# A linear-attention block times a SwiGLU block: the first 512 + 512 tokens prepared in an order written out step by step, with ScalarE normalising

## The chip, the cores and the metric

One core of one Trainium2 chip. The metric is the device time of one execution in microseconds (us). All values are float32; the matmuls take them as pairs of fp32r values (a rounded "high" part and the "low" remainder). The engines: PE multiplies matrices, DVE (VectorE), ACT (ScalarE) and POOL (GpSimd) work elementwise, SP only issues DMAs.

## The reference, cut to what matters

```python
xn = layernorm(x)                                  # x: 2048 tokens x 1024
q, k, v = heads(xn @ wqkv)                         # 32 heads of 32
pq, pk = phi(q), phi(k)                            # phi(t) = where(t > 0, t + 1, exp(t)) + 1e-6
o = (pq @ (pk^T v)) / (pq . sum(pk) + 1e-6)
s = merge(o) @ wo
g = silu((silu(xn @ w1) * (xn @ w3)) @ w2)         # w1, w3: 1024 x 3584
out = x + s * g
```

## The kernel before

The tokens are worked on in two halves of 1024. In a half, all products with the normalised rows `xn` (keys, queries, gate, up) are computed as 2x2 block products with seven instead of eight multiplications (Strassen's scheme in Winograd's form). The blocks of the left operand are 512 tokens by 512 columns: A11 and A12 are the two column halves of the first 512 tokens (row tiles `xa0` to `xa3`, 128 tokens each), A21 and A22 those of the next 512 (`xb0` to `xb3`). The seven products use

- from the rows: A11, A12, A22, S1 = A21 + A22, S2 = S1 - A11, S3 = A11 - A21, S4 = A12 - S2;
- from a pair of 128-column weight blocks: B11, B21, B22, T1 = B12 - B11, T2 = B22 - T1, T3 = B22 - B12, T4 = B21 - T2.

The pairing is B11 with A11, B21 with A12, T2 with S2, T3 with S3, T1 with S1, T4 with A22, B22 with S4. PE needs the row blocks turned: four 128x128 transposes into one PSUM bank per block and row tile (tiles `tA..`, `tS..`, line 165). Then `split` (lines 95, 96) writes the high part by an ACT cast and the low part by a DVE subtraction. One product is 12 matmuls of 128x512: four blocks of the inner dimension times three combinations of high and low (`mm3`, lines 103 to 105).

The opening of the first half is what the change touches. Rows and weights come by DMA and must be normalised, summed, turned and split before PE can multiply at full pace. `prepare_first` loads the four `xa` tiles, takes their moments on DVE, normalises them on DVE (line 158), stores them (`keep_rows`, a DMA issued by POOL, line 175) and turns A11 and A12. `Operands.made(early=True)` loads the first weight columns of a key pair (`w0k`) and makes B11 and B21; the other columns come later with the whole pair (`wk`, line 327). `gemm(early=True)` runs B11 and B21 of each of the four key pairs, since these need only the `xa` rows. `prepare_rest` loads and normalises the `xb` tiles on DVE, makes S1, S3, S2, S4 on POOL (lines 213 to 216), stores them and turns five blocks a row tile. Only then come the other five products of each pair (`bk`: T2, `ck`: T3 and T4, `dk`: T1 and B22). Tile names carry the pair: `ak` of pair 0 is `ak0_0`, written `ak__347` in the profile.

The order in which a queue holds its instructions is set by a scheduler that goes by its own estimate of times, within what the code's `issue_after` marks forbid. After the opening, `catch_up` puts one step of the waiting side work (next rows, weight sums) behind each product; that part of the code is the same in both kernels.

Of the kernel before, what the change touches and what calls it, by code (L numbers as in the profile page):

```python
# [16 lines left out]
P = 128  # L17
C = 512
# [4 lines left out]
def tile_linear_attention_times_swiglu(  # L23
# [102 lines left out]
    def load_rows(rows, name):  # L126

        t = praw.tile([P, 2, D], F32, tag="raw", name=name)
        for c, r0 in enumerate(rows):
            nc.sync.dma_start(out=t[:, c], in_=x[r0:r0 + P, :])  # L130
        return t

    def moments(xs, dst):

        bs = st.tile([P, 2, 2, nc.vector.BN_STATS_DIM], F32, tag="bs", name="bs")
        for c, t in enumerate(xs):
            gather(t, bs[:, c])
        spread(bs, dst)

# [4 lines left out]
    def spread(bs, dst):  # L144
        n = dst.shape[1]
        v, y, u = (st.tile([P, 2], F32, tag=a, name=a)[:, :n] for a in "vyu")
        for c in range(n):
            nc.vector.bn_aggr(out=dst[:, c], in_=bs[:, c])
        nc.vector.tensor_scalar_add(v, dst[:, :, 1], 1e-5)
        nc.scalar.activation(y, v, AF.Sqrt)  # L150
        nc.vector.reciprocal(y, y)

        nc.vector.tensor_mul(u, y, y)
        nc.vector.scalar_tensor_tensor(u, u, -0.5, v, op0=ALU.mult, op1=ALU.mult)
        nc.vector.scalar_tensor_tensor(dst[:, :, 1], u, 1.5, y, op0=ALU.add, op1=ALU.mult)
# [4 lines left out]
    def turn_into(A, b, i, name):  # L160

        for n, src in b.items():
            p_ = bank(f"t{n}{name}")
            for k in range(ND // 2):
                turned = nc.tensor.transpose(p_[:, k * P:(k + 1) * P], src[:, k * P:(k + 1) * P], ident)
            low = split(A[n][:, :, :, i * P:(i + 1) * P], p_.rearrange("p (k s) -> p k s", k=ND // 2))
        return turned, low

# [8 lines left out]
    def prepare_first(A, mom):  # L177

        xs = []
        for g in range(TH // 4):  # L180
            t = load_rows([(2 * g + e) * P for e in range(2)], f"xa{g}")
            xs += [t[:, e] for e in range(2)]
            for i in (2 * g, 2 * g + 1):
                moments(xs[i:i + 1], mom[:, i:i + 1])
                normalise(xs[i], mom[:, i])
                keep_rows(0, i, "A11", xs[i])
                turn_into(A, {"A11": xs[i][:, :C]}, i, f"0_{i}")
        for i, t in enumerate(xs):
            _, low = turn_into(A, {"A12": t[:, C:]}, i, f"0_{i}")
        return xs, low  # L190

    def load_second(mom, g):

        ts = []
        for i in (2 * g, 2 * g + 1):
            ts.append(job_tile([P, D], f"xb{i}") if i < 3 else pb.tile([P, D], F32, tag="b", name=f"xb{i}"))
            nc.sync.dma_start(out=ts[-1], in_=x[C + i * P:C + (i + 1) * P, :])
        j = TH // 2 + 2 * g
        moments(ts, mom[:, j:j + 2])
        return ts  # L200

    def prepare_rest(A, mom, i, t0, seconds, behind):

        with ExitStack() as order:
            for mark in behind:
                order.enter_context(tc.issue_after(mark.ins))
            if i % 2 == 0:
                seconds += load_second(mom, i // 2)
            t1, s1 = seconds[i], small(f"S1x{i}")
            normalise(t1, mom[:, TH // 2 + i])  # L210

            a11, a12, a21, a22 = t0[:, :C], t0[:, C:], t1[:, :C], t1[:, C:]
            nc.gpsimd.tensor_add(out=s1, in0=a21, in1=a22)
            nc.gpsimd.tensor_sub(out=a21, in0=a11, in1=a21)
            nc.gpsimd.tensor_sub(out=a11, in0=s1, in1=a11)
            last = nc.gpsimd.tensor_sub(out=a12, in0=a12, in1=a11)
            for n, t in (("S1", s1), ("S3", t1), ("S2", t0)):
                keep_rows(0, i, n, t)
        behind.append(last)
        yield  # L220
        turned, _ = turn_into(A, {"S2": a11, "S3": a21, "S1": s1, "A22": a22, "S4": a12}, i, f"0_{i}")
        yield turned
# [90 lines left out]
    class Operands:  # L313
# [5 lines left out]
        def __init__(self, w, c0, name, early=False, second=False):  # L319
            self.w, self.c0, self.name, self.raw, self.next = w, c0, name, None, None  # L320
            self.B, self.second = {}, second
            self.stages = self.made(early)
# [10 lines left out]

        def made(self, early):
            K = ND // 2
            b = {}

            def halves(t):
                b.update(B11=t[:, :K, :P], B21=t[:, K:, :P])

            def ready(n):
                self.B[n] = pb.tile([P, 2, K, P], FR, tag="b", name=f"{n}{self.name}")
                split(self.B[n], b[n])

            def combine(n, i0, i1, there):
                b[n] = b[there]
                nc.vector.tensor_sub(out=b[n], in0=b[i0], in1=b[i1])

            if early:
                first = pb.tile([P, ND, P], F32, tag="b", name=f"w0{self.name}")  # L350
                nc.sync.dma_start(out=first, in_=columns(self.w, self.c0, P))
                halves(first)
                ready("B11")
                ready("B21")
                yield
            self.ask()

            ahead = self.next is not None and not early
            if ahead and not self.second:
                self.next.ask()  # L360
            halves(self.raw)
            b.update(B12=self.raw[:, :K, P:], B22=self.raw[:, K:, P:])
            if early:
                combine("T1", "B12", "B11", "B11")
                ready("T1")
                combine("T2", "B22", "T1", "T1")
                ready("T2")
                yield
                combine("T3", "B22", "B12", "B12")
                ready("T3")  # L370
                yield
            else:
                ready("B11")
                yield
                combine("T1", "B12", "B11", "B11")
                combine("T3", "B22", "B12", "B12")
                ready("T3")
                yield
                combine("T2", "B22", "T1", "T3")
                ready("T2")  # L380
                yield
                ready("T1")
                yield
                ready("B21")
                yield
            combine("T4", "B21", "T2", "T2")
            ready("T4")
            yield
            ready("B22")
# [43 lines left out]
    def gemm(B, A, use, early=False, paired=False, own=False):  # L433
# [13 lines left out]
        last = product(ba, B.upto("B11"), A["A11"], True)  # L447
        copied = nc.scalar.copy(out=u, in_=ba)
        if early:
            catch_up(copied, last)  # L450
            yield
            product(ba, B.upto("B21"), A["A12"], False)
            use(0, 0, ba)
            yield
            for _ in B.stages:
# [866 lines left out]
```

## Time and profile before

| | |
|---|---|
| median of 3 runs | 2339.35 us (2336.13 to 2340.17) |
| the profiled execution | 2340.79 us, span 2339.0 us |
| PE busy | 2296.4 us, 98% of the span, 10752 matmuls |
| DVE, ACT, POOL busy | 1778.8, 926.3, 691.1 us |
| PE busy in the first 73 us | 48.96 us, clock 0.88 of full |
| PE busy from 84 to 757 us | 669.91 of 673 us, clock 1.00 |

Outside its opening PE hardly ever waits, so a microsecond less in the rest's other engines is worth nothing. In the first 73 us it waits, and part of that time it multiplies at a reduced clock. A row of the timeline gives start, duration, engine, line of the kernel, operation, tiles written and read, shape, count, and in brackets the idle time before it with what ended it. A matmul's duration is longer than the step from one matmul to the next, because matmuls overlap in the array; work on PE is counted in steps.

### The profile page before, as it was taken

Reading aid. Unit: us, or ns where it says so; the run is one execution under the profiler, and the core shown is the slowest. Engines: PE = TensorE matmul, PEld = TensorE weight load, DVE = VectorE, ACT = ScalarE, POOL = GpSimd, SP = SyncE. Lnnn points to the kernel's source line nnn. Section 1 sums busy time; section 2 is a strip of 40 time slices with the busy share of each in tenths; the row PEclk is TensorE's granted clock in tenths of the full one; section 3 lists DMA queues with packets and bytes.
Section 4 is the critical chain, followed back from the end, with each engine's and each line's share of the span. In section 5 each row is a group of like instructions: output and inputs, shape, how many; then the busy total and the mean of one; then the engine's idle time right before and its main releaser. Section 6 shows DMA issues by size and latency. Waiting matters only on the chain.

```text
span 2339.0 us, 31747 instructions
## 1 busy us (share of the span) xinstructions
PE 2296.4 (98%) x10752; PEld 1880.5 (80%) x10752; DVE 1778.8 (76%) x2830; ACT 926.3 (40%) x1639; POOL 691.1 (30%) x854
## 2 busy tenths in 40 slices
PE   6999999999999999999999999999999999999998
PEld 5788888888888888777888888888887888888876
DVE  8887898888877876567867788887755566767798
ACT  5555333433232554434243333334323634342433
POOL 4220342477676221001423435342310000000033
PEclk9999999999999999999999999999999999999999
DMA  6555556576668746776666666665756565766688
GB/s 225 179 180 178 159 178 185 173 222 216 209 217 312 248 136 200 253 257 205 213 195 194 197 195 211 200 216 168 239 171 195 165 196 172 227 205 186 190 268 269
DMA packets 353698, 479.74 MB, mean 205 GB/s; under 512 B 24208, under 2 KB 262800, under 8 KB 353424
## 3 DMA queue, kind: packets, MB, share of 16 engines
q1 hardware_dynamic: 315808, 357.63, 48.6%
q0 software_dynamic: 37728, 120.09, 15.8%
q8 instruction: 84, 1.38, 0.2%
q14 instruction: 78, 0.64, 0.1%
HBM read 306.71 MB, written 174.59 MB: 206 GB/s over the span
## 4 chain that ended last, share of the span: by engine, by line
PE 69%; DVE 6%; issue 5%; DMA 5%; ACT 1%; POOL 0%; SPq 0%; DVEq 0%; ACTq 0%; POOLq 0%
PE g L103 2%; PE g L104 2%; PE g L105 2%; PE cB L103 1%; PE cB L105 1%; PE cB L104 1%; PE dB L105 1%; PE dB L103 1%; PE dB L104 1%; PE aB L105 1%; PE aB L103 1%; PE aB L104 1%; PE bB L105 1%; PE bB L103 1%; PE bB L104 1%
## 5 line engine op out<-in xcount | busy, mean ns | idle before, releaser
L751 POOL DMA_DIRECT2D h_d<-sg x112 | 83.0, 742 | 253.0 <-DVE sg L747 166.6
L1070 POOL DMA_DIRECT2D u_d<-uB x32 | 17.4, 542 | 404.1 <-DVE uB L1053 361.1
L96 DVE TENSOR_TENSOR xy<-xy,xy 128x512 fp32r<-128x512 f32 x112 | 73.1, 686 | 64.1 <-ACT xy L95 64.1
L95 ACT CAST xy<-xy 128x512 fp32r<-128x512 f32 x112 | 65.6, 621 | 101.2 <-PE g L105 57.5
L104 PE MATMUL g<-xy,xy 128*128 128x512 f32 x224 | 87.6, 391 | 0.2 <-DVE xy L96 0.2
L105 PE MATMUL g<-xy,xy 128*128 128x512 f32 x224 | 87.1, 390 | 0.0
L103 PE MATMUL g<-xy,xy 128*128 128x512 f32 x224 | 82.6, 398 | 0.0
L518 POOL DMA_DIRECT2D y_d<-y x48 | 34.7, 724 | 140.5 <-ACT y L538 80.6
L1053 DVE TENSOR_TENSOR acc<-cB,acc 128x512 f32<-128x512 f32 x50 | 34.5, 690 | 41.2 <-PE cB L105 41.2
L1053 DVE TENSOR_TENSOR acc<-dB,acc 128x512 f32<-128x512 f32 x56 | 38.6, 689 | 29.7 <-PE dB L105 29.5
L731 POOL TENSOR_TENSOR hs<-hs,sg 128x256 f32<-128x256 f32 x56 | 60.6, 1083 | 0.1
L733 POOL TENSOR_TENSOR hs<-sg 128x256 f32<-128x256 f32 x56 | 57.6, 1029 | 0.0
L103 PEld LDWEIGHTS g<-xy,xy 128*128 128x128 f32 x224 | 41.8, 187 | 14.4 <-issue 4.1
L889 POOL DMA_DIRECT2D qs_d<-qd x32 | 18.1, 567 | 117.4 <-DVE qd L885 71.1
L1184 POOL DMA_DIRECT2D s_d<-s x32 | 17.4, 543 | 117.9 <-DVE s L1053 69.9
L730 POOL TENSOR_TENSOR hs<-sg,sg 128x256 f32<-128x256 f32 x56 | 50.3, 898 | 1.2
L734 POOL TENSOR_TENSOR hs<-sg,hs 128x256 f32<-128x256 f32 x56 | 50.0, 893 | 1.4
L104 PEld LDWEIGHTS g<-xy,xy 128*128 128x128 f32 x224 | 42.1, 188 | 9.8 <-DVE xy L96 1.2
L766 POOL TENSOR_TENSOR w<-w 128x256 f32<-128x256 f32 x28 | 27.9, 997 | 74.5 <-DMA w<-in_B_w 74.5
L105 PEld LDWEIGHTS g<-xy,xy 128*128 128x128 f32 x224 | 42.1, 188 | 8.9
L759 POOL DMA_DIRECT2D h_d<-hs x60 | 46.0, 767 | 3.5 <-POOL hs L734 2.4
L95 ACT CAST XS4B<-rS4B 128x384 fp32r<-128x384 f32 (+1 forms) x40 | 19.7, 494 | 58.8 <-PE cB L105 41.6
(5315 smaller groups left out, 8303.5 us busy)
## 6 DMA issues: line engine op xcount, KB each, us to landing
h_d<-hs POOLq DMA_DIRECT2D x60, 256.0 KB, 3.4
h_d<-sg POOLq DMA_DIRECT2D x56, 256.0 KB, 3.6
w<-in_B_w SPq DMA_DIRECT2D x56, 256.0 KB
wt_d<-w SPq DMA_DIRECT2D x28, 512.0 KB
xy<-x_d SPq DMA_DIRECT2D x28, 512.0 KB
xy<-y_d SPq DMA_DIRECT2D x28, 512.0 KB
h_d<-hs SPq DMA_DIRECT2D x52, 256.0 KB
y_d<-y POOLq DMA_DIRECT2D x48, 256.0 KB, 3.0
```

Source lines behind the costliest of these rows:

```text
L95: nc.scalar.copy(out=hi, in_=src)
L96: return nc.vector.tensor_sub(out=lo, in0=src, in1=hi.bitcast(F32))
L103: nc.tensor.matmul(acc, lhsT=wh, rhs=ah, start=start, stop=False, skip_group_check=True)
L104: nc.tensor.matmul(acc, lhsT=wh, rhs=al, start=False, stop=False, skip_group_check=True)
L105: return nc.tensor.matmul(acc, lhsT=wl, rhs=ah, start=False, stop=stop, skip_group_check=True)
L730: e.tensor_add(out=s1, in0=a21, in1=a22)
L731: e.tensor_sub(out=s2, in0=s1, in1=a11)
L733: e.tensor_sub(out=s3, in0=a11, in1=a21)
L734: e.tensor_sub(out=s4, in0=a12, in1=s2)
L751: nc.gpsimd.dma_start(out=h_d[i][2 * h + c][:, 2 * n:4 * n + 2, k], in_=src)
L759: queue.dma_start(out=h_d[i][2 * h + c][:, 6 + 4 * e:10 + 4 * e, k], in_=o[e].rearrange("p (e s) -> p e s", s=P))
L1053: return V.tensor_add(out=c, in0=src, in1=c)
```

## The change

A table `OPENING` lists every step of the opening, some 250 of them, in one sequence; a small class runs them, and inside a `manual_schedule` block the queues of PE, ACT, DVE and POOL keep that order. Beside the order, these things change:

- The rows are normalised by ACT (`do_norm`, an Identity activation with scale and shift by token; the `xa` tiles in column halves) instead of DVE, but for `xa3`, which DVE still does. DVE makes the shift. The square roots are taken for two tiles at once, and all four `xb` tiles come before the first exponential.
- S1, S3, S2 and S4 are made by DVE (but for two of the S1, on POOL). In their place POOL subtracts eleven of the low parts of weight blocks, eight before and three after the first T2 product (`glow`), which DVE did.
- The last blocks of S4 are turned during the first pair's products.
- The weights of pairs 0 and 1 come as two loads of 128 columns (`w0k`, `w1k`); the pairs' first columns come in the order 0, 3, 2, 1, and the loads of all rows are issued among them.
- B11 and B21 of a pair run as whole products, pair by pair (0, 3, 2 B11; 3, 2, 0 B21; then 1).

The diff, cut to its core:

```diff
-    def prepare_first(A, mom):
-    def load_second(mom, g):
-    def prepare_rest(A, mom, i, t0, seconds, behind):
...
+    OPENING = """
+        stat xa0; stat xa1; var a0; stat xa2; root a0; scale a0; stat xa3; norm1 xa0; high k0 B11; turn A11
+        0; norm1 xa1; var a1; low k0 B11; root a1; turn A11 1; high A11 0; scale a1; norm2 xa0; low A11 0;
...
+    LOADED = [3, 2, 1]
+
+    class Opening:
...
+            for i in range(4):
+                self.rows(f"xa{i}", i * P)
+            keys[0].fetch(self.load)
+            for k, e in zip(LOADED, range(4)):
+                keys[k].fetch(self.load)
+                self.rows(f"xb{e}", C + e * P)
+            self.rows("xb3", C + 3 * P)
...
+        def do_scale(self, g):
+            m, c = self.group(g)
+            settle(m, *self.roots[g])
+            nc.vector.scalar_tensor_tensor(self.shift[:, c], m[:, :, 0], -1.0, m[:, :, 1], op0=ALU.mult, op1=ALU.mult)
+
+        def do_vnorm(self, n):
+            normalise(self.x[n], self.mom[:, self.at(n)])
+
+        def do_norm(self, n, cols=slice(None)):
+            t, j = self.x[n][:, cols], self.at(n)
+            nc.scalar.activation(t, t, AF.Identity, scale=self.mom[:, j, 1:2], bias=self.shift[:, j:j + 1])
...
+        def do_high(self, n, i):
+            if n[0] == "k":
+                self.jobs[n, i] = self.keys[int(n[1])].place(i)
+            dst, src = self.jobs[n, i]
+            nc.scalar.copy(out=dst[:, 0], in_=src)
+
+        def do_low(self, n, i, e=nc.vector):
+            dst, src = self.jobs.pop((n, i))
+            return e.tensor_sub(out=dst[:, 1], in0=src, in1=dst[:, 0].bitcast(F32))
+
+        def do_glow(self, n, i):
+            self.do_low(n, i, nc.gpsimd)
+
+        def do_sum(self, n, i, e=nc.vector):
+            if n[0] == "k":
+                return self.keys[int(n[1])].combine(i)
+            i = int(i)
+            if n == "S1":
+                self.S1[i] = small(f"S1x{i}")
+                e.tensor_add(out=self.S1[i], in0=self.part("A21", i), in1=self.part("A22", i))
+            else:
+                a, b = {"S3": ("A11", "A21"), "S2": ("S1", "A11"), "S4": ("A12", "S2")}[n]
+                e.tensor_sub(out=self.part(n, i), in0=self.part(a, i), in1=self.part(b, i))
...
+        def do_mul(self, k, *_):
+            next(self.gemms[int(k[1])])
+
+        do_copy = do_relu = do_exp = do_phi = do_add = do_mul
...
+        def fetch(self, load):
+            first = pb.tile([P, ND, P], F32, tag="b", name=f"w0{self.name}")
+            load(first, columns(self.w, self.c0, P))
+            self.halves(first, 1)
+
+        def ask_rest(self, load):
+            self.raw = pb.tile([P, ND, P], F32, tag="b", name=f"w1{self.name}")
+            load(self.raw, columns(self.w, self.c0 + P, P))
+            self.halves(self.raw, 2)
...
-            m = [keys(pair, early=True, own=pair == 0) for pair in range(ND // 2)]
...
+            m = [keys(pair, early=True, own=pair == 0, led=pair == 0) for pair in range(ND // 2)]
+            some = mybir.EngineType
+            with tc.manual_schedule(engines={some.PE, some.Activation, some.DVE, some.Pool}):
+                last = Opening(A, early, m).run()
```

What it does to the queues is seen best on PE just ahead of the first T2 product. Before, all five blocks of the last row tile (`tS20_3`: S2 of tile 3, `xb3`, `S1x3`) stand there, S4 of every tile among them:

```order
L165 MATMUL tA220_2_669<-ident_63,xb2_468 128x128 x4
L165 MATMUL tS40_2_676<-ident_63,xa1_263 128x128 x4
L165 MATMUL tS20_3_683<-ident_63,xa1_263 128x128 x4
L165 MATMUL tS30_3_690<-ident_63,xb3_470 128x128 x4
L165 MATMUL tS10_3_697<-ident_63,S1x3_497 128x128 x4
L165 MATMUL tA220_3_704<-ident_63,xb3_470 128x128 x4
L165 MATMUL tS40_3_711<-ident_63,xa1_263 128x128 x4
L103 MATMUL bk0_0__739<-S2_0_209,T2k0_0__725 128x512
```

Now, at the same place on PE (`bk0_0` is again the T2 product of pair 0, `ak0_1` the B21 product of pair 1):

```order
L105 MATMUL ak0_1__569<-A12_0_212,B21k0_1__560 128x512
L272 MATMUL tA220_2_653<-ident_63,xb2_223 128x128 x4
L272 MATMUL tS20_2_660<-ident_63,xa1_220 128x128 x4
L272 MATMUL tA220_3_669<-ident_63,xb3_224 128x128 x4
L272 MATMUL tS40_0_675<-ident_63,xa0_219 128x128 x4
L272 MATMUL tS10_2_681<-ident_63,S1x2_558 128x128 x4
L272 MATMUL tS30_2_688<-ident_63,xb2_223 128x128 x4
L272 MATMUL tS40_3_694<-ident_63,xa1_220 128x128 x4
L103 MATMUL bk0_0__701<-S2_0_209,T2k0_0__643 128x512
```

All eight first products stand ahead of the T2 product in both, but 18 of the 20 second-row tiles are turned between them now; S4 of tiles 2 and 1 has moved behind it, the former here, between T3 and T1:

```order
L105 MATMUL ck0_0__702<-S3_0_210,T3k0_0__646 128x512
L272 MATMUL tS40_2_747<-ident_63,xa1_220 128x128 x4
L103 MATMUL dk0_0__703<-S1_0_211,T1k0_0__468 128x512
```

On POOL before, in the stretch after the four stores of the `xa` rows, the sums of one row tile stand between the stores of their results:

```order
L175 DMA x_d0_164<-xa1_263 128x1024 x2
L213 TENSOR_TENSOR S1x0_450<-xb0_430 128x512
L214 TENSOR_TENSOR xb0_430<-xa0_216,xb0_430 128x512
L175 DMA x_d0_164<-S1x0_450 128x512
L215 TENSOR_TENSOR xa0_216<-S1x0_450,xa0_216 128x512
L175 DMA x_d0_164<-xb0_430 128x1024
L216 TENSOR_TENSOR xa0_216<-xa0_216 128x512
```

Now POOL's queue at that place holds low parts of weight blocks (`B21k0_3` is B21 of key pair 3), and the only sum in it is an S1:

```order
L160 DMA x_d0_164<-xa0_219 128x1024
L284 TENSOR_TENSOR B21k0_3__365<-w0k0_3__231,B21k0_3__365 128x512
L284 TENSOR_TENSOR B11k0_2__371<-w0k0_2__234,B11k0_2__371 128x512
L284 TENSOR_TENSOR B21k0_0__374<-w0k0_0__229,B21k0_0__374 128x512
L284 TENSOR_TENSOR B11k0_1__404<-w0k0_1__237,B11k0_1__404 128x512
L160 DMA x_d0_164<-S1x1_459 128x512
L160 DMA x_d0_164<-xb1_222 128x1024
L295 TENSOR_TENSOR S1x0_502<-xb0_221 128x512
```

The sums have gone to DVE, where they stand between the low parts of the row blocks (line 284) now; a piece of DVE's queue:

```order
L284 TENSOR_TENSOR S2_0_209<-tS20_1_490,S2_0_209 128x4x128
L298 TENSOR_TENSOR xb0_221<-xa0_219,xb0_221 128x512
L298 TENSOR_TENSOR xa0_219<-S1x0_502,xa0_219 128x512
L295 TENSOR_TENSOR S1x3_531<-xb3_224 128x512
L298 TENSOR_TENSOR xb3_224<-xa1_220,xb3_224 128x512
L298 TENSOR_TENSOR xa1_220<-S1x3_531,xa1_220 128x512
L284 TENSOR_TENSOR S3_0_210<-tS30_0_526,S3_0_210 128x4x128
```

Before, DVE's queue held none of these sums; it held the normalisations of line 158 in their place.

More of the change, by code (lines that the diff above doesn't have):

```diff
@@ L192, in load_second @@
-    def load_second(mom, g):
[L194 to L200, printed above, removed]
-    def prepare_rest(A, mom, i, t0, seconds, behind):
[L204 to L222, printed above, removed]
@@ L332, in upto, with halves @@
             return self.B[n]
-        def made(self, early):
[L335 to L347, printed above, removed]
-            if early:
[L350 to L358, printed above, removed]
+        def halves(self, t, e):
+            K = ND // 2
+            self.b.update({f"B1{e}": t[:, :K], f"B2{e}": t[:, K:]})
@@ L447, in gemm @@
         last = product(ba, B.upto("B11"), A["A11"], True)
+        if early:
+            yield
         copied = nc.scalar.copy(out=u, in_=ba)
         if early:
-            catch_up(copied, last)
             yield
             product(ba, B.upto("B21"), A["A12"], False)
-            use(0, 0, ba)
             yield
-            for _ in B.stages:
-                pass
+            yield from use.steps(0, 0, ba)
+            yield
         else:
@@ L524, in use, with steps @@
         def use(n, c, src):
+            for _ in steps(n, c, src):
+                pass
+        def steps(n, c, src):
             j = 2 * pair + n
@@ L557, in turn @@
                 keep_keys(h, pair, "R6", rows["y00"])
+        use.steps = steps
         return use
@@ L697, in half @@
         if h == 0:
-            for g in m:
-                run(g)
+            with tc.issue_after(last.ins):
+                for g in m:
+                    run(g)
         else:
```

245 lines of the change are left out of this document (162 added, 83 removed).

## The prediction, made before the run

> **What bounds the kernel now.** I read the busy shares first, then the windows of the opening and of a steady stretch (length, then busy time and rows of PE, weight load, DVE, ACT, POOL, then PE's granted clock, DMA share and GB/s), then PE's waits of the first 75 us:
>
> ```profile
> PE 2296.4 (98%) x10752; PEld 1880.5 (80%) x10752; DVE 1778.8 (76%) x2830; ACT 926.3 (40%) x1639; POOL 691.1 (30%) x854
> 0.00:73.00 73.00, 48.96 (x223) 40.58 (x224) 61.29 (x132) 35.37 (x63) 30.47 (x38) 0.88 0.61 217
> 84.00:757.00 673.00, 669.91 (x3010) 553.50 (x3009) 553.91 (x783) 266.04 (x449) 319.49 (x386) 1.00 0.63 202
> PE tA L165 <- DVE v L149: 11.9, 1, 11.9
> PE bk__739 L103 <- ACT S L95: 4.7, 1, 4.7
> PE tS L165 <- DVE pk L508: 2.9, 1, 2.9
> PE tA L165 <- DVE xa L158: 1.7, 2, 0.9
> ```
>
> PE is full from 84 to 757 us and waits in the opening. So the change is worth what it takes out of the opening, less what it breaks later. PE's timeline prices PE's work:
>
> ```profile
> 11.90 1.09 PE L165 MATMUL tA<-ident,xa 128*128 128x128 f32 x4 [11.90 <-DVE v L149]
> 15.83 5.38 PE L165 MATMUL tA<-ident,xa 128*128 128x128 f32 x24 [0.80 <-DVE xa L158]
> 20.87 0.78 PE L103 MATMUL ak__347<-A,B11k__340 128*128 128x512 f32 x1
> ...
> 27.36 0.39 PE L103 MATMUL ak__347<-A,B21k__343 128*128 128x512 f32 x1
> 29.86 0.39 PE L105 MATMUL ak__347<-A,B21k__343 128*128 128x512 f32 x1
> 38.51 0.60 PE L165 MATMUL tS<-ident,xb 128*128 128x128 f32 x4
> 38.94 0.60 PE L165 MATMUL tS<-ident,S1x 128*128 128x128 f32 x4
> 65.59 0.79 PE L103 MATMUL bk__739<-S,T2k__725 128*128 128x512 f32 x1 [4.73 <-ACT S L95]
> 72.41 0.63 PE L103 MATMUL dk__741<-S,T1k__721 128*128 128x512 f32 x1
> 72.84 0.53 PE L104 MATMUL ck__740<-S,T3k__729 128*128 128x512 f32 x1
> 60.00:70.00 10.00, 4.53 (x16) 3.12 (x15) 9.20 (x16) 5.33 (x10) 0.72 (x2) 0.64 0.28 104
> ```
>
> 27.36 and 29.86 are the first and last of a product's twelve matmuls: 2.50 us for eleven steps, 0.227 each. A tile of four transposes is a step of 0.435 (38.51 to 38.94); in the first transposes, at a slow clock, 5.38 us for six tiles, 0.9 each. At 72.41 a matmul still takes 0.43.
>
> Call X the first T2 product, at 65.59. Before X stand 28 tiles (12.2 us at full clock) and eight products, 96 matmuls (21.8): 34.0 of work in 65.59, so 31.6 are lost. From X to 72.84 stand 14 matmuls, 3.2 of work in 7.25, because the 4.73 us of waiting ahead of X had let the clock fall (0.64 granted between 60 and 70): 4.1 lost. Together 35.7 us are lost. The window from 60 to 70 tells why: DVE busy 9.20 of 10, POOL 0.72. PE waits for DVE's list while POOL has nothing left. The order puts exactly the same products ahead of X after the change, but two tiles fewer.
>
> **The start.** DVE's moments, two rows of which group both halves of a tile, its small operations, and a cast on ACT:
>
> ```profile
> 5.73 1.23 DVE L142 BATCH_NORM_STATS2 bs<-xa 128x6 f32<-128x512 f32 x2
> 7.00 0.21 DVE L148 BATCH_NORM_AGGREGATE mom<-bs 128x2 f32<-128x12 f32 x1
> 7.81 1.29 DVE L142 BATCH_NORM_STATS2 bs<-xa 128x6 f32<-128x512 f32 x2 [0.60 <-DMA xa<-in_A_x]
> 10.94 0.81 DVE L158 TENSOR_SCALAR xa<-xa,mom 128x1024 f32<-128x1024 f32 x1
> 29.49 0.16 DVE L153 TENSOR_TENSOR u<-y 128x2 f32<-128x2 f32 x1
> 29.69 0.16 DVE L154 SCALAR_TENSOR_TENSOR u<-u,v 128x2 f32<-128x2 f32 x1
> 16.60 0.62 ACT L95 CAST B11k__363<-w0k__361 128x512 fp32r<-128x512 f32 x1 [0.94 <-DMA w0k__361<-in_A_wqkv]
> ```
>
> Roots for two tiles wait for the second tile's moments (5.73 + 1.23 = 6.96). The order also puts `xa2`'s moments ahead of the rest: 7.81 + 1.29 + 0.2 = 9.3. Five dependent small operations at a step of 0.2 (29.49 to 29.69): 10.3. Half a row's normalisation on ACT isn't in the trace; from below it is half of DVE's 0.81 for 1024, from above nearly the 0.62 of a 512-wide cast, which I take: 10.9. First tile turned at 11.0 instead of 11.90, a gain of 0.9. Three tiles at 0.9 end at 13.7. The fourth needs `xa3`'s moments (10.3 + 1.5), a low part (0.6), five small operations (1.0) and its normalisation (0.6): 14.4. Three more tiles: 17.1. A cast (0.6) and a low part (0.7) follow, and behind that cast on ACT stands the last half row (`norm2 xa1`); its tile and the first product come at **19.0**, where 20.87 stood.
>
> From 19.0 PE has eight products (21.8) and 18 tiles (7.8) to X: 29.6, so 48.6 if it never waits.
>
> **DVE up to X.** By the order DVE has in that stretch 37 passes of 128x512: low parts, weight sums, S sums; besides, the moments of three of the four `xb` tiles and 14 small operations.
>
> ```profile
> 60.08 0.68 DVE L347 TENSOR_TENSOR wk__718<-wk__718 128x512 f32<-128x512 f32 x1
> 60.68 0.68 DVE L96 TENSOR_TENSOR A<-tA,A 128x512 fp32r<-128x512 f32 x1
> 36.05 0.58 POOL L175 DMA_DIRECT2D x_d<-S1x  x1
> 36.65 1.31 POOL L215 TENSOR_TENSOR xa<-S1x,xa 128x512 f32<-128x512 f32 x1
> 38.46 1.29 POOL L216 TENSOR_TENSOR xa<-xa 128x512 f32<-128x512 f32 x1
> L1066 POOL TENSOR_TENSOR acc<-acc,uB 128x512 f32<-128x512 f32 x10 | 17.8, 1779 | 28.8 <-ACT acc L1211 16.1 <-DVE uB L1053 9.8 <-DVE acc L1053 2.9
> ```
>
> A pass is a step of 0.60 (60.08 to 60.68): 37 x 0.60 = 22.2; 3 x 1.4 = 4.2; 14 x 0.2 = 2.8; together 29.2. From the first product's low part at 18.4 this ends at 47.6, beside PE's 48.6. The normalisations are gone from DVE (seven of 0.81) and the POOL sums have come to it; that DVE now finishes near PE, not 17 us later, comes from the earlier start of the list, and from sums no longer waiting for POOL's chain of one tile after another (36.65, 38.46 with stores of 0.58 between).
>
> POOL gets eight low parts and two S1 ahead of X: 10 x 1.29 = 12.9, and 11 stores at 0.57, 6.3: 19.2 of about 35 us, so POOL is not the bound at that price. Its price for a subtraction with a rounded result isn't in the trace; 1.29 (38.46) is the nearest row, 1.78 the contended group's mean. The latter would make 17.8 + 6.3 = 24.1, still within 35.
>
> **DVE and POOL at once.** In the trace the two hold each other up:
>
> ```profile
> 36.93 1.05 DVE L153 TENSOR_TENSOR u<-y 128x2 f32<-128x2 f32 x1
> 38.21 2.79 DVE L155 SCALAR_TENSOR_TENSOR mom<-u,y 128x2 f32<-128x2 f32 x1
> 41.04 4.33 DVE L158 TENSOR_SCALAR xb<-xb,mom 128x1024 f32<-128x1024 f32 x2
> 600.00:620.00 20.00, 19.03 (x84) 15.46 (x83) 18.07 (x17) 5.48 (x11) 18.58 (x22) 1.00 0.71 236
> 608.52 0.68 DVE L464 TENSOR_TENSOR ug__5184<-bg__5206,ug__5184 128x512 f32<-128x512 f32 x1
> 610.90 2.46 DVE L347 TENSOR_TENSOR wu__5014<-wu__5014 128x512 f32<-128x512 f32 x1
> ```
>
> A 128x2 operation lasts 1.05 from 36.93 to 37.98, where POOL's sum of 36.65 + 1.31 ends (37.96); another lasts 2.79; a pass at 610.90 with both inputs in SBUF lasts 2.46, while one at 608.52 that reads PSUM for one input lasts 0.68. So a DVE operation with two SBUF inputs waits while POOL reads. Of the 29.2 us on DVE, 18 passes and 12 small operations (13.2, 45%) are of that kind. Bounds: none of POOL's 12.9 us meets one, cost 0; all of it does, cost 12.9. In proportion it is 45%, **5.8 us**. If instead every such pass met POOL as the one at 610.90 did (1.78 over 0.68, in a window with POOL busy 18.58 of 20, where here its operations fill 12.9 of 35), it would be 18 x 1.78 x 0.37/0.93 = 12.7, the upper end again. I take the proportional value, since neighbouring passes there, as at 608.52, lost nothing. So X comes at 47.6 + 5.8 + 0.6 for the last cast and turn = **54**.
>
> [...]
>
> **After X.** 14 matmuls (3.2), two S4 tiles moved there (0.9) and 1.5 for short waits bring PE at 59.6 to where it stood at 72.84: 13.2 us gained. The matmuls behind X need DVE's low part of the last S2 tile and POOL's of T2; a wait for either is in the 1.5. [...]
>
> [...]
>
> Loads:
>
> ```profile
> 25.10 0.63 ACT L95 CAST B11k__409<-w0k__407 128x512 fp32r<-128x512 f32 x1
> 18.57 0.37 SPq L351 DMA_DIRECT2D w0k__407<-in_A_wqkv  x1
> 759.97 0.50 PE L103 MATMUL bk__6503<-S,T2k__6354 128*128 128x512 f32 x1 [1.49 <-ACT T2k__6354 L95]
> ```
>
> Pair 0's second columns are asked for once POOL has done `B21k3` (about 21.5); a load asked for at 18.57 was used at 25.10, so it takes at most 6.5 us, 28.0. DVE wants it for T1 at about 27: 0 to 1 us, inside the 1.5. ACT loses nothing: its windows above show it about half busy. Later the code is the same with its order shifted a little, so I count one more wait like the row at 759.97 (1.5). Gain 13.2 - 1.5 = **11.7**.
>
> **Rivals.**
> R1, the strict lock: every microsecond of POOL's 12.9 falls on a DVE operation, 7.1 more than counted: 2334.8. For it, the 2.46 at 610.90; against it, DVE's 55% of other operations go on meanwhile.
> R2, slower: POOL's rounding subtraction has no row and takes d us. PE's products need these low parts, eight before X, so each costs d - 1.3 once POOL is full. POOL's spare time is 35 - 19.2 = 15.8; the gain is spent when 8 x (d - 1.3) exceeds 15.8 + 11.7, from d = 4.7 on. At d = 6 it is 37.6 - 15.8 = 21.8 lost against the forecast: 2349.5. Against it: rounding costs DVE nothing (0.68 at 60.08 without, 0.68 at 60.68 with it).
> R3, nothing waits: X near PE's own 48.6, 5.4 more gain: 2322.3. For it, POOL could fall beside DVE's PSUM reads.
> R4, the rest gives back 5: later sums and T4 are made when POOL is busy, as at 600 to 620, and waits like 759.97 come three more times: 2332.7.
> That the table isn't kept is excluded by the order, which shows it on all four queues.
>
> **How the numbers follow.** The profiled execution took 2340.79 us (span 2339.0), 1.44 above the median of the runs shown and just outside them. 2340.79 - 11.7 = 2329.1; carried to the median, 2339.35 - 11.7 = **2327.7**. Chances: forecast 0.52 (its own range 2324 to 2331), R1 0.14, R2 0.10, R3 0.12, R4 0.12. About 0.2%, 4.7 us, is what a measurement of this kernel can tell from no change, so faster means below 2334.7. The forecast, R3, half of R1 and two thirds of R4 are faster: 0.52 + 0.12 + 0.07 + 0.08 = 0.79. The rest of R1 and R4, 0.11, is the same, R2's 0.10 slower. The range reaches from a little under R3 to a little over R1, 2320 to 2337, and leaves R2 and a few extremes out.
>
> **What would show it.** Right: first transposes at about 11, first product near 19, X near 54, no PE wait over 2 us between 19 and X, 0.39-long matmuls right behind X, POOL subtractions near 1.3, DVE sums between 0.6 and 2, and no new PE waits from 84 to 757. Wrong in one term: X after 60 with DVE full and sums over 2 (R1); PE waiting for a POOL low part (R2); X under 50 (R3); PE waits of several us later (R4). A first product after 21 would put the start wrong, with whatever ACT holds there as the cause.

## The result, and the profile after

| | before | after |
|---|---|---|
| median of 22 runs each | 2339.22 us (2334.34 to 2343.51) | 2334.24 us (2328.17 to 2336.82) |
| the profiled execution | 2340.79 us, span 2339.0 | 2331.29 us, span 2329.5 |

The ratio is 0.9977 (95% interval 0.9972 to 0.9983): 5.0 us faster. Forecast were 11.7 us. The direction was right, the size was not half of it. 2334.24 is near what R4 (2332.7) and R1 (2334.8) gave. R1 it wasn't, since the first T2 product came well before 60; R4's mechanism has a part in it.

Busy shares and two windows of the changed kernel, in the same columns as before:

```profile
PE 2290.6 (98%) x10752; PEld 1873.7 (80%) x10752; DVE 1773.4 (76%) x2820; ACT 929.1 (40%) x1645; POOL 681.6 (29%) x851
```

```profile
0.00:73.00 73.00, 53.61 (x272) 43.13 (x273) 63.99 (x136) 43.39 (x75) 26.68 (x35) 1.00 0.62 217
84.00:757.00 673.00, 669.03 (x3000) 551.70 (x2999) 558.35 (x781) 267.51 (x454) 324.58 (x394) 1.00 0.64 206
```

In the opening PE is busy 4.7 us more and its granted clock is full where it was 0.88 (its record begins at 16.2 us, that of before at 21.9; ahead of that a transpose steps by 0.21 us in both kernels, where later it steps by 0.11). From 84 to 757 us it idles 4.0 us where it idled 3.1. PE's waits and its timeline:

```profile
PE tA L272 <- ACT xa L261: 12.7, 4, 11.4
PE tS L272 <- DVE A L284: 4.3, 2, 3.0
PE bk__6806 L103 <- ACT T2k__6622 L95: 1.3, 1, 1.3
```

```profile
11.40 1.09 PE L272 MATMUL tA<-ident,xa 128*128 128x128 f32 x4 [11.40 <-ACT xa L261]
...
18.79 0.47 PE L103 MATMUL ak__350<-A,B11k__268 128*128 128x512 f32 x1
...
48.06 1.16 PE L272 MATMUL tS<-ident,S1x 128*128 128x128 f32 x8 [2.98 <-DVE A L284]
...
56.57 0.50 PE L103 MATMUL bk__701<-S,T2k__643 128*128 128x512 f32 x1
56.91 0.39 PE L104 MATMUL bk__701<-S,T2k__643 128*128 128x512 f32 x1
```

The first tile is turned at 11.40 (forecast 11.0), the first product runs at 18.79 (19.0), the first T2 product X at 56.57 (54), and the matmul behind X takes 0.39, at a granted clock of 1.00. The start holds, X is 2.6 us late, and ahead of X stands a wait of 2.98 us. Its cause stands in DVE's and POOL's timelines:

```profile
43.95 3.37 DVE L284 TENSOR_TENSOR T1k__468<-w0k__229,T1k__468 128x512 fp32r<-128x512 f32 x1
47.24 1.27 DVE L284 TENSOR_TENSOR A<-tA,A 128x512 fp32r<-128x512 f32 x2
...
53.27 0.69 DVE L632 SCALAR_TENSOR_TENSOR pk<-ak__350,pk 128x512 f32<-128x512 f32 x1 [0.97 <-ACT pk L630]
...
55.23 0.69 DVE L284 TENSOR_TENSOR A<-tA,A 128x512 fp32r<-128x512 f32 x1 [1.07 <-ACT A L280]
55.84 0.68 DVE L284 TENSOR_TENSOR S<-tS,S 128x512 fp32r<-128x512 f32 x1
```

```profile
44.26 1.28 POOL L284 TENSOR_TENSOR B21k__560<-w0k__237,B21k__560 128x512 fp32r<-128x512 f32 x1
45.49 1.26 POOL L284 TENSOR_TENSOR B22k__582<-w1k__395,B22k__582 128x512 fp32r<-128x512 f32 x1
```

DVE's low part of T1, both inputs in SBUF, lasts 3.37 instead of 0.69: it ends at 47.32, 0.57 after POOL's two subtractions (to 46.75), as if it had begun only then. Behind it in DVE's queue stand the low parts of A22 (47.24), which free the PSUM banks that PE's next tiles need.

Where time went in the whole program I read from PE's records: from the start of PE's k-th matmul I take 0.2266 us for each 512-wide matmul before it and 0.109 for each transpose (0.435/4) and each narrower one. The rest is lost time. In the last part this price does not fit the narrower matmuls, so the differences count there, not the sign. The order of the last part (from the 3862nd matmul) is the same in both kernels. Three profiles of each kernel (the second and third from runs described below):

```
                      lost up to the 300th   300th to 3862nd     3862nd to the last
before                36.0  35.3  35.5       8.6   5.5   7.8     -39.1 -38.9 -40.0
after                 24.7  25.9  24.4       9.5  10.8  11.1     -37.7 -38.2 -38.2
gain of the means     10.6                   -3.2                -1.3
```

10.6 - 3.2 - 1.3 = 6.1; the means of the three spans (2337.2 and 2331.0) differ by 6.2. The forecast had 13.2 for the first column and -1.5 for the other two.

### The profile page after: what moved, and what is told of

Its sections match the earlier page's. It is cut to its first block, busy times and chain, and to the rows that moved or that the text cites. A ratio compares the mean times of both kernels' runs of the same rounds, so it can differ in the third digit from the quotient of the medians.

```text
span 2329.5 us, 31760 instructions
## 1 busy us (share of the span) xinstructions
PE 2290.6 (98%) x10752; PEld 1873.7 (80%) x10752; DVE 1773.4 (76%) x2820; ACT 929.1 (40%) x1645; POOL 681.6 (29%) x851
## 4 chain that ended last, share of the span: by engine, by line
PE 59%; DVE 4%; DMA 3%; issue 1%; ACT 1%; SPq 0%; DVEq 0%; ACTq 0%
PE g L103 2%; PE g L104 2%; PE g L105 2%; PE cB L103 1%; PE dB L105 1%; PE dB L103 1%; PE cB L105 1%; PE dB L104 1%; PE cB L104 1%; PE aB L105 1%; PE aB L104 1%; PE aB L103 1%; DMA rA22B<-h_d 1%; PE bB L103 1%; PE bB L105 1%
## 5 line engine op out<-in xcount | busy, mean ns | idle before, releaser
L642 POOL DMA_DIRECT2D y_d<-y x48 | 34.9, 727 | 117.1 <-ACT y L666 69.6
L1174 DVE TENSOR_TENSOR acc<-dB,acc 128x512 f32<-128x512 f32 x56 | 38.5, 688 | 30.1 <-PE dB L105 29.9
L104 PEld LDWEIGHTS g<-xy,xy 128*128 128x128 f32 x224 | 42.1, 188 | 10.6 <-DVE xy L96 1.5
L798 POOL DMA_DIRECT2D pq_d<-pq x32 | 17.5, 547 | 104.5 <-DVE pq L632 104.3
```

What stands on the lines that cost most here:

```text
L104: nc.tensor.matmul(acc, lhsT=wh, rhs=al, start=False, stop=False, skip_group_check=True)
L1174: return V.tensor_add(out=c, in0=src, in1=c)
```

## The experiments

**The same kernels again.** No edit. Two theories of the 3 us between the profiled execution and the median:

> The changed kernel unchanged, for a second profile and more times with PE's granted clock of each. The profiled execution took 2331.29 us with a mean granted clock of 0.999, and its first T2 product came at 56.6 us as forecast (54), yet the median of 22 runs is 2334.24. Theory A (clock): in most executions PE's waits of the opening (3.0 us at 45 to 48 above all) let the clock fall, which the first profile happened to escape. Then a profile with a mean clock of 0.997 or 0.998 shows matmul steps of 0.43 instead of 0.227 somewhere before 75 us, 5 to 10 us of them, and the time of a run goes with its clock, about 2.3 us for each 0.001. Rival B (later waits): the opening is the same in every execution, and the 3 us lie in PE's waits behind 300 us, at the change of halves (740 to 790) above all; then steps in the opening stay at 0.227 and the later waits grow by 3 us or more.

> The kernel before unchanged, for a second profile and the clock of each run. [...] Rival B: its opening is the same to 0.5 us and its spread comes from later waits.

Medians 2334.72 (11 runs) and 2338.24 (10). The second profile of the changed kernel (2333.59 us), PE's timeline behind the wait and two windows:

```profile
47.94 1.94 PE L272 MATMUL tS<-ident,S1x 128*128 128x128 f32 x8 [2.98 <-DVE A L284]
49.53 0.78 PE L103 MATMUL ak__569<-A,B21k__560 128*128 128x512 f32 x1
50.10 0.63 PE L104 MATMUL ak__569<-A,B21k__560 128*128 128x512 f32 x1
50.53 0.63 PE L105 MATMUL ak__569<-A,B21k__560 128*128 128x512 f32 x1
50.95 0.43 PE L103 MATMUL ak__569<-A,B21k__560 128*128 128x512 f32 x1
```

```profile
45.00:55.00 10.00, 7.06 (x38) 6.38 (x39) 7.77 (x12) 4.79 (x9) 3.90 (x4) 0.83 0.28 111
745.00:755.00 10.00, 7.99 (x27) 5.83 (x26) 9.91 (x10) 5.09 (x10) 7.72 (x9) 0.83 1.03 376
```

After the same 2.98 us wait the clock falls here and matmuls step by 0.43 (50.10 to 50.53); in the first profile, and in the third, they don't (granted from 45 to 55: 0.83 here, 1.00 there). Once more it falls at the change of halves (745 to 755, granted 0.83), where seven steps of 0.43 cost 1.4 us. So both theories hold a part: the clock is one source of the spread, with about as much at the change of halves (1.4 us) as in the opening (1.2 more lost up to the 300th matmul). Among the 22 runs the two at a mean clock of 0.999 took 2328.2 and 2331.3, the ten at 0.998 2333.9 in the median, the eight at 0.997 2335.1, the two at 0.996 2332.9 and 2336.8. In the 11 runs of the second series the time does not go with the clock: 2333.4 at 0.999, but 2333.2 and 2336.1 at 0.996. The kernel before is nearer to rival B: its opening differs by 0.7 us between profiles, its later waits by 3.2.

**The pass that collided.** In the list of steps (here and below cut to the steps that change):

```diff
-        0; low k0 T1; exp k3;
+        0; exp k3;
-        phi k0; high A22 2;
+        phi k0; low k0 T1; high A22 2;
```

> DVE's low part of T1 of pair 0, which took 3.37 us at 43.95 behind two POOL subtractions, stands ten steps later, behind the feature map of pair 0, where DVE was idle; nothing else changes. Theory A: PE's wait of 3.0 us before the S1 tiles of rows 0 and 3 falls to under 0.6, the first T2 product comes 2 to 2.7 us sooner (near 54), the clock stays at full in more executions, and the median falls by 3 to 6 us, to 2328 to 2331. Rival B: only the wait goes, the median falls by 2 to 2.7 us, to 2331.5 to 2332.3. If later waits take it all back, the median stays at 2334.

T1's low part is taken from a block here that T2's sum has overwritten, so this part of the computation is another; the operations are the same. X came at 53.37, 3.2 us sooner, lost time to the 300th matmul was 21.5 (25.0 in the mean of the changed kernel), the median 2331.24, between what theory A and rival B had. PE's wait in the place was gone. That is more than the 2.7 that the pass lasts too long, but the pass itself also stands now where DVE had idled. The run with both edits, further down, keeps it among the busy passes and loses 22.7 up to the 300th matmul: by it the collision alone costs the opening 2.3 us.

**POOL's low parts back to DVE.**

```diff
-        B11; high k3 B21; low k3 B11; high A12 3; low A12 2; glow k3 B21; high k2 B11; low A12 0; high k0
+        B11; high k3 B21; low k3 B11; high A12 3; low A12 2; low k3 B21; high k2 B11; low A12 0; high k0
...
```

and so at all eleven places.

> The eleven low parts that the change gave to POOL go back to DVE, at the same places of the list. My sum for the opening holds that POOL's eight before the first T2 product cost DVE 5.8 us of blocked passes (the traces show 2.7 in one pass and some 3 in small ones), and DVE would pay 8 x 0.60 = 4.8 for doing them itself. So by my terms it comes out about even: first T2 product within 2 us of 56.6, the median 2333 to 2337. If POOL's parts cost DVE nearly nothing but the one pass, it is slower by 2 to 4 us in the opening (2336 to 2339).

A miss: X at 54.42, lost time 22.6, median 2329.88 (ratio to before 0.9964, 0.9950 to 0.9979), so 4.8 us under the changed kernel on the same chip (2334.72) and not even with it. The T1 pass in DVE's timeline, and X in PE's:

```profile
43.82 0.68 DVE L284 TENSOR_TENSOR T1k__468<-w0k__229,T1k__468 128x512 fp32r<-128x512 f32 x1
```

```profile
54.42 0.50 PE L103 MATMUL bk__701<-S,T2k__643 128*128 128x512 f32 x1
```

DVE does 4.8 us more before X and yet is done sooner. From 18.3 us to X its steps add up to 34.9 us here and to 34.8 in the changed kernel, but it idles 1.0 instead of 3.4. So this part of the change costs time in the opening: what POOL takes from DVE's list it gives back in held-up passes, and more through what waits for them. The opening explains 2.4 of the 4.8. Between the 300th and the 3862nd matmul this profile lost 12.4, more than the changed kernel's, so where the rest of the 4.8 comes from is not shown.

**One place of the second half in its old order.** Line 95's cast of T2 for the second key pair of the second half, on ACT and DVE:

```diff
-                phi(src, pq)
+                with ExitStack() as held:
+                    if (h, pair, n, c) == (1, 0, 1, 0):
+                        held.enter_context(tc.issue_after(cast["k1_1_"].ins))
+                    phi(src, pq)
...
```

`cast` keeps the instruction that casts a pair's T2. In the same way the copy of `k1_1_` and the two operations that make `y10` and R5 of pair 0 are held behind T2's cast and low part.

> The changed kernel, with one place of the unchanged second half put back into the order that it had in the kernel before: on ACT the copy of the B11 product, the turned keys' bias and the feature map of the last query block stand behind the cast of the next key pair's T2, on DVE the difference R5 behind T2's low part. In both profiles of the changed kernel PE waits 1.3 us there (near 786), in both of the kernel before it doesn't. Theory O (the order of the rest): the wait goes, the second half starts its next pair 1.3 us sooner, and the median falls by 1.0 to 1.6, to about 2333.2. Rival: the engines are late there whatever the order, because the queries of the pair come late; then the wait moves to the next product and the median stays at 2334.5.

In the changed kernel PE waits for this cast, and the cast stands behind a copy and a bias; first PE's and then ACT's timeline:

```profile
787.24 0.50 PE L103 MATMUL bk__6806<-S,T2k__6622 128*128 128x512 f32 x1 [1.33 <-ACT T2k__6622 L95]
```

```profile
785.51 0.59 ACT L556 COPY uk__6776<-ak__6777 128x512 f32<-128x512 f32 x1 [0.45 <-PE ak__6777 L105]
785.99 0.69 ACT L673 ACTIVATE y<-trk,tiny 128x512 f32<-128x512 f32 x1
786.57 0.62 ACT L95 CAST T2k__6622<-wk__6558 128x512 fp32r<-128x512 f32 x1
```

With the old order restored, the same matmul in PE's timeline has no wait ahead of it:

```profile
786.70 0.60 PE L644 MATMUL trk<-ident,pk 128*128 128x128 f32 x4
787.39 0.50 PE L103 MATMUL bk__6806<-S,T2k__6622 128*128 128x512 f32 x1
```

The third profile of the changed kernel comes to the same place at the same time:

```profile
786.72 0.60 PE L638 MATMUL trk<-ident,pk 128*128 128x128 f32 x4
788.65 0.50 PE L103 MATMUL bk__6806<-S,T2k__6622 128*128 128x512 f32 x1 [1.33 <-ACT T2k__6622 L95]
```

From the 3300th to the 3500th matmul the three profiles of the changed kernel lost 2.2, 1.8 and 1.8 us, those of before 0.2, this one 0.5. So the written opening changes what the scheduler does 700 us later, in code that the diff doesn't touch, and at this place that costs 1.3 us: shown. That the whole program gets it back is not shown. The median was 2332.83 (0.9968, 0.9958 to 0.9979), 1.4 to 1.9 under the changed kernel, but on another chip, the interval overlaps the changed kernel's (0.9972 to 0.9983), and the profiled execution (2333.54) is no shorter than the mean of the changed kernel's three (2332.8).

**Both edits**, with T1's low part ahead of T2's sum this time:

```diff
-        0; low k0 T1; exp k3;
+        0; exp k3;
-        sum k0 T2; high S2 3;
+        high S2 3;
-        low S2 3; high S1 3;
+        low S2 3; low k0 T1; sum k0 T2; high S1 3;
```

> The edit of the run before (one place of the second half in the old order) and in the opening DVE's low part of T1 behind the low part of S2 of tile 3, with the weight sum of T2 right behind it, where POOL has no subtraction left to hold it up. The pass of 3.37 us falls to about 0.7, PE's wait of 3.0 us to under 0.6. By waits alone: 2.6 from the opening and 1.3 from the second half, 2334.5 to 2330.6. If the slow clock behind that wait also cost time in most executions (0.4 to 2 us), 2328.5 to 2330.2. If it is all given back later, 2333 or more.

2329.02 us (0.9961, 0.9949 to 0.9974), within the range of 2328.5 to 2330.2. In DVE's timeline the pass lasts 0.68, at 47.29; X comes at 54.51, where the forecast had 54:

```profile
47.29 0.68 DVE L284 TENSOR_TENSOR T1k__468<-w0k__229,T1k__468 128x512 fp32r<-128x512 f32 x1
```

```profile
54.51 0.50 PE L103 MATMUL bk__701<-S,T2k__643 128*128 128x512 f32 x1
```

Its five runs (2328.57 to 2330.76) lie under all of the kernel before and under all but 2 of the 33 of the changed kernel; the intervals of the two ratios still touch. The low parts on DVE together with the second half's old order does as well:

> All low parts on DVE again, and the one place of the second half in the old order: the two edits that each made the changed kernel faster (2329.9 and 2332.8). Adding them, the wait of 1.3 us at the second half goes from the run with the low parts on DVE: 2328.5, 10.5 us under the kernel before. If later waits give it back, 2329.9.

2329.47 (0.9954, 0.9940 to 0.9967), only 0.4 under the run with the low parts alone, nearer to 2329.9 than to 2328.5. The three best versions can't be told apart by their intervals.

**What each part of the change is worth.** Three parts undone, one profile each; the single times were 2337.05, 2338.27 and 2337.83 us, all between the changed kernel's and the kernel before's medians. The normalisation back on DVE:

```diff
-        norm1 xa0
...
-        norm2 xa0
...
-        norm xb1
+        vnorm xa0
...
+        vnorm xb1
...
```

> One part undone: DVE normalises all eight row tiles, whole, at the places where ACT did. DVE gets seven passes of 0.8 more, 5.2 us, on the list that ends last; ACT loses about 8. If DVE's list sets the opening, the first T2 product and the 300th matmul come 4 to 6 us later than in the changed kernel (56.6 and 78.5 to 79.8 there). If the order alone brought the gain and ACT's part none, they come within 1 us.

X at 60.59, 4.0 later and at the lower end of what I had expected; lost time 28.7, 3.7 more than the changed kernel, and 1.6 of it are eight steps of 0.43 behind a wait of 3.49 (granted 0.89 from 45 to 60). S4 ahead of T2:

```diff
-        mul k0 T2; low S4 0; high S4 3; low S3 2;
+        low S4 0; high S4 3; low S3 2;
...
+        turn S4 2; high S4 2; turn S4 1; high S4 1; low S4 2; low S4 1; keep S2 2; keep S2 1; mul k0 T2;
```

> One part undone: all of S4 is summed, turned and split ahead of the first T2 product, as before the change. That puts two sums, two low parts (4 x 0.6 on DVE) and two tiles (0.9 on PE) ahead of it. Expected: the first T2 product 2.5 to 4 us later (59 to 61), the 300th matmul 1.5 to 3 us later, since the same DVE work then is gone behind it. If what stands behind T2 on DVE is the bound anyway, the 300th matmul stays where it is.

A miss upward: X at 64.03, lost time 31.9, 6.9 more. PE's waits and its timeline there:

```profile
PE tS L247 <- DVE A L259: 4.3, 2, 3.0
PE tS L247 <- DVE xa L273: 3.0, 1, 3.0
```

```profile
62.44 1.94 PE L247 MATMUL tS<-ident,xa 128*128 128x128 f32 x8 [3.03 <-DVE xa L273]
64.03 0.78 PE L103 MATMUL bk__726<-S,T2k__643 128*128 128x512 f32 x1
64.61 0.63 PE L104 MATMUL bk__726<-S,T2k__643 128*128 128x512 f32 x1
65.03 0.63 PE L105 MATMUL bk__726<-S,T2k__643 128*128 128x512 f32 x1
```

S4's sums come last on DVE, PE has nothing else to do (3.03), and then multiplies at the slow clock, seven steps of 0.43 that cost 1.4 us (granted 0.72 from 58 to 70). That is the state of the kernel before, in small. But not all of the 6.9 is S4's. Nine more steps of 0.43 stand from 50.3 us on, behind the wait that the changed kernel has too (3.00 here; granted 0.77 from 45 to 60). Through them ACT's cast of T3 and the feature map come late, and DVE idles 3.41 for it, where it idled 0.97. The last tile ahead of S4's, at 55.98 in the changed kernel, comes at 58.76: 2.8 us were gone before the edit had any part in it. The sums back on POOL and all low parts on DVE:

```diff
-        sum S1 1; sum S3 1;
+        gsum S1 1; gsum S3 1;
...
-        glow k3 B21;
+        low k3 B21;
...
```

> One part undone: POOL makes all sixteen S sums and DVE all low parts, in the same list. POOL's sums take 1.3 us each and follow one another within a tile, DVE's 0.7. If the exchange of the engines is what lets DVE's list end near PE, the lost time of PE up to its 300th matmul (24.7 and 25.9 us in the changed kernel, 36 in the kernel before) rises by 3 to 6 us. If the written order alone did it, it stays within 1 us of 25.

Lost time 30.3, 5.2 more, as expected. Against the run with only the low parts moved (22.6) the sums alone are worth 7.6, a spell of slow steps from 54.6 to 64.4 us included (0.88 for a tile at 54.58, 0.43 for a matmul at 62.25). The three add up to 15.8, more than the gain of 10.6: they come from one profile each, all three with a spell of slow clock, and are not shares of the gain. What the written order is worth by itself was not run. That the second weight columns come by loads of their own wasn't tried alone: whole pairs need the buffers that hold the `xa` rows until S4 is made.

**The tail.**

> A third profile of the kernel before, for the part of the program whose order is the same in both kernels on every engine: from PE's 3862nd matmul to the last it took 39.1 and 38.9 us less than a fixed price for each matmul in two profiles of the kernel before, and 33.6 to 38.3 less in eight profiles of kernels with the new opening, 37.0 in the mean. Theory O (everything that is given back is order): no difference by kernel there, so this one lies anywhere between 34 and 39. Rival T (the tail itself is slower): 38.5 to 39.5.

> A third profile of the changed kernel. Lost time of PE up to its 300th matmul 24.7 and 25.9 us so far: again 24 to 26.5, with or without a spell of 0.43 steps behind the wait of 3.0 us near 45. Between the 300th and the 3862nd it lost 9.5 and 10.8 us so far, the kernel before 8.6 and 5.5: again 9 to 11, with the wait of 1.3 us at 786 among them. In the tail, by theory O anywhere between 34 and 39, by rival T 36 to 38.

The single times were 2338.74 and 2333.42; the profiles are the third column of the table above. In the tail before had -40.0 (past rival T's 38.5 to 39.5, and past theory O's 34 to 39 too), the changed kernel -38.2, but the run with the sums on POOL, whose order there is the changed kernel's, -40.6, and the kernels with the new opening as a whole -33.6 to -40.6. So no difference by kernel is shown there; the 1.3 us in the means stays open.

## Why the prediction was right or wrong

**Right.** The start: 11.40 and 18.79, for 11.0 and 19.0. POOL's subtraction with a rounded result: 1.28, for 1.29, so R2 falls. The time that DVE's passes lose to POOL: 2.7 in the T1 pass, 1.4 in a small operation at 32.65, 0.9 at 25.41 and 0.4 at 41.11, together 5.4 for 5.8 (4.5 in the second profile, where the one at 25.41 is not held up). No slow clock right behind X (a matmul of 0.39 at 56.91, granted 1.00). DVE's rows, and POOL's pass beside the first of them:

```profile
25.41 1.23 DVE L140 TENSOR_SCALAR v<-mom 128x2 f32<-128x2 f32 x2
32.65 1.58 DVE L147 TENSOR_TENSOR u<-y 128x2 f32<-128x2 f32 x1
41.11 1.11 DVE L298 TENSOR_TENSOR xa<-xa 128x512 f32<-128x512 f32 x1
25.26 1.29 POOL L284 TENSOR_TENSOR B11k__404<-w0k__237,B11k__404 128x512 fp32r<-128x512 f32 x1 [1.04 <-ACT B11k__404 L280]
```

Two things in it differ from the prediction's reading. The rows at 32.65 and 41.11 meet POOL's S1 sums, not its low parts; they are held up as much in the run with the low parts on DVE. And the operation at 25.41 reads one tile only: the first of the two lasts 1.16, to the end of POOL's pass (26.55), so two inputs in SBUF are not the only case that waits.

The start came out for a reason that is partly another:

```profile
13.99 3.44 PE L272 MATMUL tA<-ident,xa 128*128 128x128 f32 x20 [0.16 <-ACT xa L261]
18.38 0.66 PE L272 MATMUL tA<-ident,xa 128*128 128x128 f32 x4 [0.95 <-ACT xa L261]
```

The five tiles from 13.99 on took 3.44, not 4.5: up to 16.2 us a transpose is a step of 0.21, behind it one of 0.11. The 0.9 a tile was too much for the later ones. It made no difference, because the last tile waited 0.95 for ACT's last half row.

**Wrong, first step: "So X comes at 47.6 + 5.8 + 0.6 for the last cast and turn = 54".** X came at 56.6, 57.8 and 56.3. The sum of the list held: DVE's steps from 18.3 us to X add up to 34.8, for 29.2 + 5.8. What failed is that I spread the 5.8 evenly over a list that never idles: DVE idled 3.4. Half of the 5.8 fell into one pass, with the low parts that free PE's banks behind it. PE stood 2.98 us, its next tiles came later, ACT's casts of them too, and DVE then idled 0.97 and 1.07 us (53.27, 55.23) for what it had itself held up; another 0.68 went to a row tile that came late (its moments, at 23.85). I had bounded the sum of the cost, not its place. With that pass moved X came at 54.51. That this is near the forecast's 54 is luck: DVE's steps then add up to 32.1, and it idles 3.8, 1.90 of it ahead of the moved pass. "no PE wait over 2 us between 19 and X" fell with it: behind the wait of 2.98 to 2.99 the clock fell in one of three profiles (granted 0.83 from 45 to 55 there, 1.00 in the others). That the 14 matmuls behind X run at full clock was the author's estimate; the first profile shows it (0.39 at 56.91, steps of 0.23).

**Wrong, second step: "Later the code is the same with its order shifted a little, so I count one more wait".** I counted 1.5; the profiles show 3.2 from the 300th to the 3862nd matmul, and 4.5 with the tail. One wait of 1.3 us at 786 is shown to be order (the run with the old order there). A second small one is as regular: at the change of halves the third matmul of the first T2 product waits 0.7 us for the low part before and 1.1 after, the same in all three profiles of each kernel. PE's waits, before and then after:

```profile
PE bk__6503 L105 <- DVE T2k__6354 L96: 0.7, 1, 0.7
```

```profile
PE bk__6502 L105 <- DVE T2k__6329 L96: 1.1, 1, 1.1
```

The rest I can place but not settle: from the 300th to the 1400th matmul the changed kernel lost 1.0 less; from the 1400th to the 2200th (320 to 505 us) 1.5 us more, for a wait near 485 on a DVE sum (0.5 in two of the three profiles of before, 0.7, 1.2 and 1.5 in the changed one); from the 2200th to the 3300th 0.8 more, the 0.4 just named among them and the spells of slow clock behind it (granted 0.83 from 745 to 755 in the second and third profiles), which reach past the 3300th. The 1.3 of the tail is in the means and not shown to belong to the kernels. R4 named this mechanism and gave it 5 us; its chance of 0.12 was too low.

**The carry to the median.** The forecast set one profiled execution's gain against the median. The three profiled executions of the changed kernel took 2332.8 in the mean, the median of its 33 runs is 2334.3; those of the kernel before are at its median. That is another 1.6, on the side of the changed kernel alone. Spells of slow clock could make it (in the first series the lower clocks go with the longer times, in the second they don't), but none of the profiled executions was above 2334, so no profile shows it and the cause stays open.

Sum: 11.7 - 2.6 (X) - 3.0 (given back beyond the 1.5 counted) - 1.6 (carry) = 4.5, against 5.0 measured.

## What to carry to other kernels

A cost that comes from two engines meeting is to be placed, not only summed: look which instruction stands behind the one that is held up, and who waits for that. Where a scheduler orders the code behind a change, its order is part of the change; compare it up to the point where both are the same, and price what moved ahead of each wait. An operation given to a second engine, whose passes hold up those of the first, may cost more than it takes off: DVE was sooner at X with eight more passes of its own (X at 54.42) than beside POOL's (56.57).

## What the runs showed of the hardware

In these runs the clock's fall is not tied to one length of wait. Behind the same wait of 2.98 to 3.00 us it fell in the second profile of the changed kernel and in the one with S4 ahead (granted 0.83 from 45 to 55 and 0.77 from 45 to 60), and it stayed in the first and third profiles of the changed kernel (1.00). At the change of halves it fell behind two waits of 1.0 and 0.7 in the third profile of before (0.83 from 755 to 765) and stayed behind 1.5 and 0.7 in the first; in the changed kernel it fell behind 0.9 and 1.1 in the second profile (0.83 from 745 to 755) and stayed behind 1.1 and 1.1 in the first. In the first profile of before every change of the recorded clock lies a whole number of 3.413 us behind the start of the record at 21.9 us (7, 9, 12, 15 and 677 of them), in that of the changed kernel the only change does (676, from 16.2 us). PE's busy time in stretches of this length (length, busy time and rows of PE, granted clock, DMA share, GB/s), first two of the second profile of the changed kernel, then two of the first, then two pairs of the first profile of before:

```profile
44.21:47.62 3.41, 0.74 (x7) 1.00 1.02 400
47.62:51.03 3.41, 3.09 (x12) 0.50 0.04 16
```

```profile
43.47:46.88 3.41, 1.61 (x12) 1.00 0.97 370
46.88:50.29 3.41, 2.23 (x14) 1.00 0.31 123
```

```profile
42.39:45.81 3.42, 0.82 (x4) 1.00 0.49 192
45.81:49.22 3.41, 2.46 (x11) 0.50 0.42 171
59.46:62.87 3.41, 1.40 (x13) 1.00 0.84 340
62.87:66.29 3.42, 0.70 (x1) 0.50 0.01 1
```

Nearly the whole wait of 2.98 falls into one stretch in the second profile (0.74 busy), and the clock is at half in the next; in the first profile a border cuts the wait in two (1.61 and 2.23 busy), and the clock stays. In before the clock is at half behind stretches with 0.82 and 1.40 busy. Up to the last 10 us these are the only two falls in the first profiles of the two kernels, and no other stretch at full clock has less than 1.61 busy. So the same wait cost no slow step in one profile, and steps of 0.43 in another.

ACT's normalisation of half a row takes 0.81 us, above the 0.62 of a cast of the same shape that I took:

```profile
10.49 0.81 ACT L261 ACTIVATE xa<-xa,shift,mom 128x512 f32<-128x512 f32 x1 [2.80 <-DVE shift L254]
```
